# Turning the attention keys by 32 x 32 blocks on VectorE in a kernel of linear attention and two MLP layers

## The chip, the cores and the metric

One Trainium2 chip, one of its cores. The time is the device time of one launch in microseconds. The kernel before takes 914.3 us, the median of three runs (913.77 to 916.93).

## The reference

Linear attention with a decaying state (4 batches B, 8 heads H, 768 steps S, head size D of 48), then two MLP layers over the 3072 x 384 result, with a hidden width of 2048. Cut to what is computed:

```python
for t in range(S):                      # state: B, H, D, D
    cur = einsum('bhd,bhe->bhde', u * k[t], v[t])
    y[t] = einsum('bhd,bhde->bhe', r[t], state + cur)
    state = w[t][..., None] * state + einsum('bhd,bhe->bhde', k[t], v[t])
x = y.transpose(0, 2, 1, 3).reshape(B * S, H * D)        # 3072 x 384
h = x @ w_in;   x = (h * clip(h + 3, 0, 6) / 6) @ w_out  # layer 1
h = x @ w_in2;  x = (h * sigmoid(h)) @ w_out2            # layer 2
```

The MLP weights arrive as 64-bit floats, seen as pairs of 32-bit words, and are turned into 32-bit floats on the chip.

## The kernel before

**Groups and chunks.** The 768 steps are cut into 6 chunks of 128. A chunk of one batch is a group: 24 groups, group g being batch g % 4 of chunk g // 4. `attention(g, key)` (L588) handles one group with its 8 heads as 4 pairs, a pair on partitions 0 to 47 and 64 to 111 of a tile. Per group:

- VectorE scans the decay ws forward into `pre` (L600) and backward into `suf` (L607; `indq` between them is a reciprocal of four values), and multiplies them with r and k from `rk`: `rh` (L612), `kh` (L615).
- TensorE forms the scores `pa` of kh and rh (L625, 16 products), and turns kh with four matmuls against the identity into `pk` (L638). ScalarE copies pk to `khn` (L642).
- `bb` holds the sums of r u k by head. In groups 0 to 3 VectorE multiplies r and k (`rkp`, L646), and TensorE sums them against `u_bd` (L653). Later, GpSimd makes `ruk` (L659) and VectorE sums it (L666).
- ScalarE writes two tiles `a` that hold bb on their diagonals (L680), and VectorE puts pa above the diagonal with a masked copy (L683).
- TensorE forms the outputs `py` from the state, a and v (L696). ScalarE copies them to x (L714), and VectorE takes the rest that the copy lost (L717; not in chunk 0).
- For the state, TensorE multiplies khn and v to `pkv` (L728). The state `s` becomes (s + pkv) x `grown`, where grown is a copy of four columns of pre (L734). This is done on VectorE (L745, L746), and in groups 0 to 3 by eight activations on ScalarE (L754).

The last chunk (groups 20 to 23) needs no new state, so no pk, khn or pkv.

**MLP layers.** The four groups of a chunk are 512 tokens. `block1` (layer 1) and `block2` (layer 2) go over 16 slices fc of the hidden width. `mm1` makes h (L831) and `mm2` adds to three output sums, acc in layer 1 and acd in layer 2 (L851). Each product is made of three: both factors are split into a rounded part and a rest (wh, wl; xh, xl; gh, gl), so 9 matmuls for h and 9 for the sums. In chunk 0, the first 8 slices use the unsplit weights and x ("whole"; L821, L842), one matmul each. Between the two products ScalarE applies Relu (L882) or Silu (L921), VectorE the min and product (L884), a cast makes gh (L861 or L862, on either engine), and a subtraction on VectorE gl (L864).

**Weights.** `load_w` loads a slice's 64-bit words into `raw` (two buffers), VectorE decodes them in three steps (`upper_bits`, `sign_bits`, `lower_bits`), and ScalarE and VectorE split them (L488, L489) into one of 17 slots `w`. While these slots are empty, attention tiles of groups 1 to 3 live in them (names `spare` and `home`).

**What sets the order.** Nothing is scheduled by hand or by the compiler: every piece is an `Op` with a cost in ns for each engine that may run it, a key, and the tiles that it reads and writes. `Plan.order` is a list scheduler. It simulates the five engines, one DMA channel, the buffers, and a port that VectorE and GpSimd share (`port=True`), takes again and again the op that can start first (the lowest key among those), and writes out a fixed order for each engine. All DMAs are issued from SyncE's queue in this order. So a changed cost moves instructions elsewhere. `keep_busy` adds filler matmuls with a very high key, which run on TensorE before the first weight matmul where nothing else is ready. Groups 0 to 3 have keys below -96 and run first; groups 4 j to 4 j + 3 run among the MLP work of chunk j - 1.

Of the kernel before, what the change touches and what calls it, by code (L numbers as in the profile page):

```python
# [344 lines left out]
def tile_decay_attention_mlp2(  # L345
# [81 lines left out]
    indq = Part(ap_.tile([PD, SEQ + 1], F32, name="indq"))  # L427
    causal = Part(ap_.tile([128, C], F32, name="causal"))
    u_bc = Part(ap_.tile([128, H, D], F32, name="u_bc"))
    u_bd = Part(ap_.tile([PD, NP, 2], F32, name="u_bd"))  # L430
    stray = Part(stray_t)

    def fill_ind(e):
# [18 lines left out]
    wts, vals = {}, {}  # L452
    WBUFS = 17

    def load_w(layer, fc, key, where="wp", after=(), whole=False):
        src = (m1, m2)[layer]
        nm = f"{layer}_{fc}"
        raw = Part(new("cst", "raw", 2, [128, 2, DM, WW], f"raw{nm}", I32))
        op({"SP": 470}, key - 3, lambda e: e.dma_start(
            out=raw.ap.rearrange("p a f t -> p (a f t)"), in_=src[fc]  # L460
        ), writes=[raw], data=1150.0 * WW, after=after)
        if whole:
            if fc % 2 == 0:
                vals[fc] = new("wp", "w", WBUFS, [128, 2, 2, DM], f"val{nm}")
            val = Part(vals[fc - fc % 2], lambda t: t[:, fc % 2])
            bits = val
        else:
            bits = Part(new("cst", "bits", 1, [128, 2, DM], f"bits{nm}"))
            val = bits
        if WW == 2:  # L470
            op({"DVE": 480}, key, lambda e: upper_bits(e, raw.ap, val.ap.bitcast(I32)), [raw], [val])
# [62 lines left out]
    def load_group(g, key, after=()):  # L534
        first = 0 < g < B
        slots = {}

        def home(tag, shape, at, slot, kind="wp"):
            if not first or g == 1 and tag != "rk":
                return Part(new("np", tag, 1 if tag == "rk" else 2, shape, f"{tag}{g}"))  # L540
            if slot not in shared:
                shared[slot] = new("wp", "w", WBUFS, [128, 4 * DM], f"home{slot}")
            n = 1
            for x in shape[1:]:
                n *= x
# [10 lines left out]
        parts = [(ws, wseq_in, 700.0), (rk, rk_in, 1400.0), (vn, v_in, 700.0)]  # L556
        rkn = None
        if g >= B:
            rkn = Part(new("np", "rkn", 2, [128, 2 * H, D], f"rkn{g}"))
            parts.append((rkn, rkn_in, 1200.0))  # L560
        for p, src, data in parts:
            op({"SP": 470}, key, lambda e, p=p, src=src: e.dma_start(
                out=p.ap.rearrange("p a b -> p (a b)") if len(p.ap.shape) == 3 else p.ap,
                in_=src[g],
            ), writes=[p], data=data, after=after)
        return ws, rk, vn, rkn
# [8 lines left out]
            op({"PE": cost}, 1e6, run, [ident], [filler])  # L575

    filler = Part(new("ps", "h", 2, [128, 256], "filler"))
    keep_busy(16, 430)
    keep_busy(24, 300)

    states = {}
    x_parts = {}
    first_scores = []
# [4 lines left out]
    def attention(g, key):  # L588
# [7 lines left out]
        def of(t, i, n):  # L596
            return t.ap[:, i * n:(i + 1) * n, :]
# [10 lines left out]
            flat(suf)[:, ::-1], ws.ap[:, 1:SEQ + 1][:, ::-1], indq.ap[:, 1:SEQ + 1][:, ::-1],  # L608
            0.0, op0=ALU.mult, op1=ALU.add,
        ), [ws, indq], [suf], port=True)  # L610
        rh, kh = att("rh", [PD, NP, C], g), att("kh", [PD, NP, C], g)
        op({"DVE": 610}, key, lambda e: e.tensor_tensor(  # L612
            rh.ap, of(rk, 0, NP), pre.ap[:, :, 0:C], op=ALU.mult
        ), [rk, pre], [rh], port=True)
        op({"DVE": 610}, key, lambda e: e.tensor_tensor(  # L615
            kh.ap, of(rk, 1, NP), suf.ap[:, :, 1:SEG], op=ALU.mult
        ), [rk, suf], [kh], port=True)

        pa = [att_ps([128, NP, C], f"pa{i}_", g) for i in range(2)]
# [10 lines left out]
        o_scores = op({"PE": 1090}, key, scores, [kh, rh], pa)  # L630
        if g == 2:
            first_scores.append(o_scores)
        if not last:
            pk = att_ps([128, NP, PD], "pk", g)

            def back(e):
                for p in range(NP):
                    e.transpose(pk.ap[:, p, :], kh.ap[:, p, :], ident.ap[:PD, :PD])  # L638

            op({"PE": 500}, key, back, [kh, ident], [pk])  # L640
            khn = att("khn", [128, NP, PD], g)
            op({"ACT": 490}, key, lambda e: e.activation(khn.ap, pk.ap, AF.Copy), [pk], [khn])  # L642

        if first:
            rkp = att("rkp", [PD, NP, C], g)
            op({"DVE": 600}, key - 0.05, lambda e: e.tensor_tensor(  # L646
                rkp.ap, of(rk, 0, NP), of(rk, 1, NP), op=ALU.mult
            ), [rk], [rkp], port=True)
            bb = att_ps([128, H, 1], "bb", g)

            def sums(e):
                for p in range(NP):
                    e.matmul(bb.ap[:, 2 * p:2 * p + 2, 0], rkp.ap[:, p, :], u_bd.ap[:, p, :],  # L653
                             start=True, stop=True)

            op({"PE": 790}, key - 0.05, sums, [rkp, u_bd], [bb])
        else:
            ruk = att("ruk", [128, H, D], g)
            op({"POOL": 1000}, key, lambda e: e.tensor_tensor(  # L659
                ruk.ap, of(rkn, 0, H), u_bc.ap, op=ALU.mult  # L660
            ), [rkn, u_bc], [ruk], port=True)
            op({"POOL": 1000}, key, lambda e: e.tensor_tensor(
                ruk.ap, ruk.ap, of(rkn, 1, H), op=ALU.mult
            ), [ruk, rkn], [ruk], port=True)
            bb = Part(new("ap", "bb", 2, [128, H, 1], f"bb{g}"))
            op({"DVE": 540}, key, lambda e: e.tensor_reduce(  # L666
                flat(bb), ruk.ap, axis=AX.X, op=ALU.add
            ), [ruk], [bb])
# [6 lines left out]
        for i in range(2):  # L675
            a = att("a", [128, NP, C], g, str(i), bufs=2)

            def diagonal(e, a=a, i=i):
                for p in range(NP):
                    e.activation(a.ap[:, p, :], ident.ap, AF.Copy, scale=bs.ap[:, 2 * p + i])  # L680

            op({"ACT": 1000}, key, diagonal, [bs, ident], [a])
# [31 lines left out]
        op({"ACT": 490}, key, lambda e: e.activation(xh.ap[:, :, sl], py.ap, AF.Copy), [py], [xh])  # L714
        if j not in WHOLE:
            xl, = xl
            op({"DVE": 560}, key, lambda e: e.tensor_tensor(  # L717
# [3 lines left out]
        if not last:  # L721
# [3 lines left out]
            def outer_kv(e):  # L725
# [5 lines left out]

            op({"PE": 500}, key, outer_kv, [khn, vn], [pkv])
            grown = Part(new("ap", "grown", 2, [PD, NP, 1], f"grown{g}"))
            op({"DVE": 100}, key, lambda e: e.tensor_copy(grown.ap, pre.ap[:, :, C:SEG]),  # L734
               [pre], [grown])
            now = state
            if not state:
                now = Part(new("ap", f"s{o}", 1, [PD, NP, 2 * D], f"s{g}"))
# [19 lines left out]
            if state:  # L758
                op({"DVE": 1440}, key, grow, [pkv, now, grown], [now], port=True)
            else:  # L760
                op({"ACT": 1700}, key + 2.0, first_grow, [pkv, now, grown], [now])
            states[o] = now


# [70 lines left out]
            op({"PE": 681}, key, run, [wh, wl, xh, xl], [h])  # L835
        return h

    def mm2(layer, fc, gh, gl, acc, key):
        wh, *wl = wts[layer, fc]
        for c in range(KC):  # L840
            if not wl:
# [70 lines left out]
    def block2(j, key):  # L912
# [4 lines left out]
        for fc in range(FC):  # L917
# [2 lines left out]
            g = Part(new("gp", "g", 2, [128, N], f"g2_{j}_{fc}"))  # L920
            op({"ACT": 595}, kk, lambda e, g=g, h=h: e.activation(g.ap, h.ap, AF.Silu), [h], [g])  # L921
            gh, gl = split(g, f"2_{j}_{fc}", kk, {"DVE": 430}, {"DVE": 690})
            mm2(1, fc, gh, gl, acc, kk + MM2)
        for c in range(KC):
            o = Part(new("late", "o", 3, [128, N], f"o{j}_{c}"))
            op({"ACT": 595, "DVE": 690}, key + FC, lambda e, c=c, o=o: (
# [167 lines left out]
```

## Time and profile before

| | |
|---|---|
| median of the runs | 914.3 us |
| the profiled execution | 914.26 us |
| its span (first to last instruction) | 912.5 us |
| mean granted TensorE clock | 0.996 of full speed |
| HBM read, written | 90.75 MB, 9.44 MB: 110 GB/s |
| share of the chain that ended last: TensorE, VectorE, DMA, ScalarE | 88%, 8%, 2%, 1% |

In the profile PE is TensorE's matmul, PEld its weight load (which overlaps matmuls), DVE is VectorE, ACT ScalarE, POOL GpSimd and SPq the DMA queue of SyncE. The ends of pipelined matmuls are modelled, so for TensorE the distance between two starts is the surer figure. A row of a timeline gives the start and duration in us, the engine, the line, the operation and the tiles (out<-in), the shapes and how many instructions of one kind stand together; in brackets how long the engine was idle before, and for what. A name such as x, w or h stands for all its numbered buffers.

### The profile page before, as it was taken

What the parts mean: (1) busy time and instruction counts of PE and PEld (TensorE: products, weight loads), DVE (VectorE), ACT (ScalarE), POOL (GpSimd) and SP (SyncE); (2) the same over time, 40 slices, a digit from 0 to 9 for tenths busy, and PEclk for the clock granted to TensorE, in tenths of its full rate; (3) what the DMA queues carried; (4) which work ended last, traced back from release to release, by engine and by line L of the source; (5) the groups of instructions that cost most, each with busy time, mean ns of one, the idle gap of its engine ahead of it and who ended that gap; (6) DMA issues with size and microseconds to landing.
All of it is one profiled execution on the core that took longest, in us unless ns stands there. A gap on an engine that the chain in (4) does not pass through costs nothing.

```text
span 912.5 us, 13679 instructions
## 1 busy us (share of the span) xinstructions
PE 902.0 (99%) x5554; PEld 720.6 (79%) x5554; DVE 574.4 (63%) x942; ACT 324.6 (36%) x694; POOL 61.8 (7%) x52
## 2 busy tenths in 40 slices
PE   8999999999999999999999999999999999999997
PEld 7546788887888888888888888888888888888886
DVE  8999999867785776664468878544544633222221
ACT  5524474423432333322146765323232311212111
POOL 1203112311120211000000000000000000000000
PEclk9999999999999999999999999999999999999999
DMA  9765433322321221110066764634645500100101
GB/s 277 235 214 185 133 109 117 97 65 93 88 87 29 96 69 41 66 32 1 24 226 215 229 215 168 239 112 167 208 139 173 173 1 1 35 1 5 31 1 36
DMA packets 39603, 101.10 MB, mean 111 GB/s; under 512 B 3697, under 2 KB 16113, under 8 KB 39537
## 3 DMA queue, kind: packets, MB, share of 16 engines
q1 hardware_dynamic: 39536, 100.20, 34.2%
q8 instruction: 44, 0.72, 0.3%
q14 instruction: 23, 0.18, 0.1%
HBM read 90.75 MB, written 9.44 MB: 110 GB/s over the span
## 4 chain that ended last, share of the span: by engine, by line
PE 88%; DVE 8%; DMA 2%; ACT 1%; issue 1%; SPq 0%; DVEq 0%; ACTq 0%
PE h L831 40%; PE acd L851 21%; PE acc L851 19%; PE py L696 3%; PE pa L625 2%; PE pk L638 1%; DVE val L38 1%; DMA raw<-in_moe_w_dram 1%; PE pkv L728 1%; DVE g L884 1%; DVE bits L44 1%; DVE bits L38 1%; DVE val L44 1%; DVE pre L600 1%; DVE suf L607 0%
## 5 line engine op out<-in xcount | busy, mean ns | idle before, releaser
L831 PE MATMUL h<-x,w 128*128 128x512 f32 x1584 | 391.3, 390 | 0.0
L831 PEld LDWEIGHTS h<-x,w 128*128 128x128 f32 x1584 | 296.0, 188 | 62.2 <-issue 0.6
L851 PE MATMUL acd<-gh,w 128*128 128x512 f32 x576 | 192.9, 389 | 0.0
L862 DVE CAST gh<-g 128x512 fp32r<-128x512 f32 x150 | 64.9, 433 | 197.8 <-ACT g L921 194.2
L851 PE MATMUL acc<-gh,w 128*128 128x512 f32 x528 | 180.6, 393 | 0.3 <-ACT x L891 0.3
L921 ACT ACTIVATE g<-h 128x512 f32<-128x512 f32 x96 | 57.4, 599 | 264.3 <-PE h L831 242.8
L864 DVE TENSOR_TENSOR gl<-g,gh 128x512 fp32r<-128x512 f32 x184 | 130.1, 707 | 4.7 <-ACT gh L861 0.3
L851 PEld LDWEIGHTS acd<-gh,w 128*128 128x128 f32 x576 | 108.1, 188 | 22.3
L882 ACT ACTIVATE g<-h 128x512 f32<-128x512 f32 x96 | 57.2, 596 | 190.0 <-PE h L831 172.9
L851 PEld LDWEIGHTS acc<-gh,w 128*128 128x128 f32 x528 | 99.1, 188 | 22.8 <-issue 1.0
L884 DVE SCALAR_TENSOR_TENSOR g<-g,h 128x512 f32<-128x512 f32 x96 | 65.3, 682 | 77.6 <-ACT g L882 77.3
L851 PE MATMUL acd<-gl,w 128*128 128x512 f32 x288 | 112.1, 389 | 0.0
L851 PE MATMUL acc<-gl,w 128*128 128x512 f32 x264 | 103.1, 391 | 0.0
L851 PEld LDWEIGHTS acd<-gl,w 128*128 128x128 f32 x288 | 54.1, 188 | 11.3
L851 PEld LDWEIGHTS acc<-gl,w 128*128 128x128 f32 x264 | 49.6, 188 | 10.2 <-DVE gl L864 0.5
L659 POOL TENSOR_TENSOR ruk<-rkn,u_bc 128x384 f32<-128x384 f32 x20 | 36.1, 1807 | 288.4 <-DVE bb L666 250.1
L680 ACT ACTIVATE a<-ident,bb 128x128 f32<-128x128 f32 x160 | 49.6, 390 | 3.2 <-DVE bb L666 3.2
L683 DVE COPY_PREDICATED a<-causal,pa 128x512 f32<-128x512 int32 x42 | 29.1, 731 | 8.0 <-PE pa L625 8.0
L789 DVE TENSOR_SCALAR_CACHE_REDUCE cval<-cval 128x768 f32<-128x768 f32 x32 | 30.3, 946 | 2.3 <-ACT cval L28 2.3
L773 ACT ACTIVATE off<-cw 112x512 f32<-112x512 f32 x48 | 30.3, 631 | 1.8 <-DMA cw<-in_wseq_dram 0.9
L28 ACT ACTIVATE cval<-craw 128x768 f32<-128x768 f32 x32 | 28.8, 901 | 0.0
L600 DVE TENSOR_TENSOR_SCAN pre<-ws,ind 112x516 f32<-112x516 f32 x21 | 26.5, 1263 | 1.9 <-DMA ws<-in_wseq_dram 1.9
(105 smaller groups left out, 714.5 us busy)
## 6 DMA issues: line engine op xcount, KB each, us to landing
raw<-in_moe_w_dram SPq DMA_DIRECT2D x32, 768.0 KB, 4.7
craw<-in_moe_w_dram SPq DMA_DIRECT2D x32, 768.0 KB, 4.4
rk<-in_rk_dram SPq DMA_DIRECT2D x21, 448.0 KB, 3.9
rkn<-in_rkn_dram SPq DMA_DIRECT2D x20, 384.0 KB, 3.2
cw<-in_wseq_dram SPq DMA_DIRECT2D x24, 226.2 KB, 3.4
ws<-in_wseq_dram SPq DMA_DIRECT2D x22, 226.2 KB, 2.8
vn<-in_vn_dram SPq DMA_DIRECT2D x22, 224.0 KB, 2.6
x2d<-x SPq DMA_DIRECT2D x18, 256.0 KB, 2.4
```

Of the source, the lines that this page charges most:

```text
L600: op({"DVE": 1150}, key, lambda e: e.tensor_tensor_scan(flat(pre), ws.ap[:, 0:SEQ], ind.ap[:, 0:SEQ], 0.0, op0=ALU.mult, op1=ALU.add), [ws ...
L659: op({"POOL": 1000}, key, lambda e: e.tensor_tensor(ruk.ap, of(rkn, 0, H), u_bc.ap, op=ALU.mult), [rkn, u_bc], [ruk], port=True)
L680: e.activation(a.ap[:, p, :], ident.ap, AF.Copy, scale=bs.ap[:, 2 * p + i])
L773: e.activation(off.ap, ws.ap[:, 0:SEQ].rearrange("p (a b) -> p a b", b=SEG)[:, :, 1:], AF.Relu, scale=sign, bias=-W_REACH - sign, accum_ou ...
L789: op({"DVE": 600}, key, lambda e: e.tensor_scalar(val.ap, val.ap, TINY, 0.0, op0=ALU.is_lt, op1=ALU.add, accum_out=stray.ap[:, col:col + 1 ...
L831: e.matmul(h.ap, a.ap[:, 0, kc * 128:(kc + 1) * 128], b.ap[:, kc, :], start=(kc == 0 and i == 0), stop=(kc == KC - 1 and i == 2),)
L851: e.matmul(acc[c].ap, a.ap[:, 1, sl], b.ap, start=(fc == 0 and i == 0), stop=(fc == FC - 1 and i == 2),)
L862: else e.tensor_copy(gh.ap, src.ap)
L864: op(lo_engs, key, lambda e: e.tensor_tensor(gl.ap, src.ap, gh.ap.bitcast(F32), op=ALU.subtract), [src, gh], [gl], port=True)
L882: op({"ACT": 595}, kk, lambda e, g=g, h=h: e.activation(g.ap, h.ap, AF.Relu, bias=3.0), [h], [g])
L884: op({"DVE": 690}, kk, lambda e, g=g, h=h: e.scalar_tensor_tensor(g.ap, g.ap, 6.0, h.ap, op0=ALU.min, op1=ALU.mult), [g, h], [g])
L921: op({"ACT": 595}, kk, lambda e, g=g, h=h: e.activation(g.ap, h.ap, AF.Silu), [h], [g])
```

## The change

- For groups 9 to 19 the four matmuls pk and the copy khn go. VectorE transposes kh into khn with 16 instructions a group, each turning one 32 x 32 block of each of the four pairs (`turn`). For this kh has 128 partitions; ScalarE zeroes the upper 32. `TURN_FROM = 9` sets the first such group.
- In groups 4 to 8 the sums bb go from one VectorE reduction to eight activations with an accumulator on ScalarE (`total_by_head`). The copies `grown` go from VectorE to ScalarE in all groups.
- In layer 1, raw words of slices 2 to 9 are loaded into free slots w, up to four slices ahead.
- The first 24 instead of 16 fillers, of two matmuls each, are planned at 330 ns instead of 430.
- The buffer of u_bd is taken through the plan, and the first DMA is planned 450 ns longer; group 3's state is planned behind its copy of py to x.
- In the last chunk of layer 2, the keys of the last three slices' output sums are changed, so that the sums end one after another.
- Some planned durations of DMAs, of the diagonals and of upper_bits are changed.

```diff
@@ load_w
+    RAW_AHEAD = 4
+    def new_raw(layer, fc):
+        nm = f"raw{layer}_{fc}"
+        if layer == 0 and 2 <= fc < 10:
+            return Part(new("wp", "w", WBUFS, [128, 4 * DM], nm), ...)
+        return Part(new("cst", "raw", 2, [128, 2, DM, WW], nm, I32))
-        raw = Part(new("cst", "raw", 2, [128, 2, DM, WW], f"raw{nm}", I32))
+        if layer == 0:
+            for x in range(fc, min(fc + RAW_AHEAD, FC)):
+                if x not in raws:
+                    raws[x] = new_raw(0, x)
+        raw = raws.pop(fc) if layer == 0 else new_raw(layer, fc)
@@ fillers
-    keep_busy(16, 430)
+    keep_busy(24, 330)
     keep_busy(24, 300)
+    TURN_FROM = 9
@@ attention
-        rh, kh = att("rh", [PD, NP, C], g), att("kh", [PD, NP, C], g)
+        rh, kh = att("rh", [PD, NP, C], g), att("kh", [128 if g < 1 or g >= B else PD, NP, C], g)
+        if g >= TURN_FROM and not last:
+            op({"ACT": 500}, key, lambda e: e.activation(
+                kh.ap[96:], ident.ap[96:].unsqueeze(1).to_broadcast([32, NP, C]), AF.Copy, scale=0.0
+            ), [ident], [kh])
...
-        if not last:
+        if not last and g >= TURN_FROM:
+            khn = att("khn", [128, NP, 128], g)
+
+            def turn(e, i, j):
+                e.transpose(
+                    khn.ap[j * 32:(j + 1) * 32, :, i * 32:(i + 1) * 32],
+                    kh.ap[i * 32:(i + 1) * 32, :, j * 32:(j + 1) * 32],
+                )
+
+            for i in range(4):
+                for z in range(4):
+                    op({"DVE": 195}, key, lambda e, i=i, z=z: turn(e, i, z), [kh], [khn])
+        elif not last:
             pk = att_ps([128, NP, PD], "pk", g)
...
-            op({"DVE": 540}, key, lambda e: e.tensor_reduce(
-                flat(bb), ruk.ap, axis=AX.X, op=ALU.add
-            ), [ruk], [bb])
+            def total_by_head(e):
+                for h in range(H):
+                    e.activation(ruk.ap[:, h], ruk.ap[:, h], AF.Copy, accum_out=bb.ap[:, h])
+
+            if g < 9:
+                op({"ACT": 1900}, key, total_by_head, [ruk], [ruk, bb])
+            else:
+                op({"DVE": 540}, key, lambda e: e.tensor_reduce(
+                    flat(bb), ruk.ap, axis=AX.X, op=ALU.add
+                ), [ruk], [bb])
...
-            op({"DVE": 100}, key, lambda e: e.tensor_copy(grown.ap, pre.ap[:, :, C:SEG]),
-               [pre], [grown])
+            op({"ACT": 200}, key, lambda e: e.activation(
+                grown.ap, pre.ap[:, :, C:SEG], AF.Copy
+            ), [pre], [grown])
...
-                op({"ACT": 1700}, key + 2.0, first_grow, [pkv, now, grown], [now])
+                op({"ACT": 1700}, key + 2.0, first_grow, [pkv, now, grown], [now],
+                   after=[o_x] if g == B - 1 else ())
@@ block2
-            mm2(1, fc, gh, gl, acc, kk + MM2)
+            turn = {FC - 3: (-0.5, 0.05, 0.1), FC - 2: (0.2, 0.3, 1.4), FC - 1: (1.2, 1.3, 1.5)}
+            mm2(1, fc, gh, gl, acc, kk + MM2, [
+                key + FC - 1 + x for x in turn.get(fc, ())
+            ] if j == NCH - 1 else ())
```

The order of the instructions moves in three places that matter below. VectorE's queue in the head, before (group 0's scan, then its products; `spare1` and `home1` belong to group 1):

```order
L600 SCALAR_TENSOR_TENSOR pre_0_142<-ws0_101,ind_84 112x516
L603 RECIPROCAL indq_85<-pre_0_142 112x4
L734 COPY grown0_155<-pre_0_142 112x4
L646 TENSOR_TENSOR rkp_0_157<-rk0_109 112x512
L607 SCALAR_TENSOR_TENSOR suf_0_165<-ws0_101,indq_85 112x516
L612 TENSOR_TENSOR rh_0_177<-rk0_109,pre_0_142 112x512
L615 TENSOR_TENSOR kh_0_190<-rk0_109,suf_0_165 112x512
```

and in the changed kernel:

```order
L617 SCALAR_TENSOR_TENSOR pre_0_148<-ws0_99,ind_84 112x516
L620 RECIPROCAL indq_85<-pre_0_148 112x4
L624 SCALAR_TENSOR_TENSOR suf_0_165<-ws0_99,indq_85 112x516
L679 TENSOR_TENSOR rkp_0_180<-rk0_103 112x512
L633 TENSOR_TENSOR rh_0_186<-rk0_103,pre_0_148 112x512
L636 TENSOR_TENSOR kh_0_195<-rk0_103,suf_0_165 112x512
```

The copy of grown has gone, and the backward scan stands ahead of rkp, the first instruction that needs rk. VectorE's queue in chunk 1, between the masked copy of group 9 and the rest gl of slice 4, before:

```order
L683 COPY_PREDICATED a1_9_1609<-causal_86,pa1_9_1629 128x512
L884 SCALAR_TENSOR_TENSOR g1_4_1637<-g1_4_1637,h0_1_4_1603 128x512
L603 RECIPROCAL indq_85<-pre_10_1639 112x4
L666 TENSOR_REDUCE bb10_1699<-ruk_10_1599 128x8
L607 SCALAR_TENSOR_TENSOR suf_10_1703<-ws10_1391,indq_85 112x516
```

and in the changed kernel, where slice 4 is handled:

```order
L658 STREAM_TRANSPOSE khn_9_1660<-kh_9_1503 32x4x32
L930 SCALAR_TENSOR_TENSOR g1_4_1743<-g1_4_1743,h0_1_4_1688 128x512
L658 STREAM_TRANSPOSE khn_9_1660<-kh_9_1503 32x4x32
L908 CAST gh1_4_1767<-g1_4_1743 128x512
L658 STREAM_TRANSPOSE khn_9_1660<-kh_9_1503 32x4x32
L910 TENSOR_TENSOR gl1_4_1773<-g1_4_1743,gh1_4_1767 128x512
L658 STREAM_TRANSPOSE khn_9_1660<-kh_9_1503 32x4x32
L707 TENSOR_REDUCE bb10_1782<-ruk_10_1647 128x8
L658 STREAM_TRANSPOSE khn_9_1660<-kh_9_1503 32x4x32
L930 SCALAR_TENSOR_TENSOR g1_5_1779<-g1_5_1779,h0_1_5_1755 128x512
```

Nearly every transposition stands between two instructions of other kinds, and the cast gh is on VectorE. TensorE's queue at group 12, before:

```order
L625 MATMUL pa0_12_2244<-rh_12_2092,kh_12_2034 128x128
L625 MATMUL pa1_12_2246<-rh_12_2092,kh_12_2034 128x128
L638 MATMUL pk12_2256<-ident_83,kh_12_2034 128x112 x4
L831 MATMUL h0_2_0_2262<-x0_0_2_1519,w0_0_1312 128x512
L831 MATMUL h0_2_0_2262<-x1_0_2_1535,w0_0_1312 128x512
```

and in the changed kernel:

```order
L646 MATMUL pa0_12_2328<-rh_12_2187,kh_12_2240 128x128
L646 MATMUL pa1_12_2330<-rh_12_2187,kh_12_2240 128x128
L875 MATMUL h0_2_0_2341<-x0_0_2_1557,w0_0_1382 128x512
L875 MATMUL h0_2_0_2341<-x1_0_2_1582,w0_0_1382 128x512
L875 MATMUL h0_2_0_2341<-x0_0_2_1557,w0_0_1382 128x512 x2
```

The four turning matmuls pk12 have gone, and the weight matmuls follow the scores.

## Rows read from the trace of the kernel before

**Rows 1.** The page, part 1: busy us, share of the span and instructions.

```profile
PE 902.0 (99%) x5554; PEld 720.6 (79%) x5554; DVE 574.4 (63%) x942; ACT 324.6 (36%) x694; POOL 61.8 (7%) x52
```

**Rows 2.** Timeline of TensorE, 29 to 33 us; start and duration first.

```profile
30.43 1.08 PE L696 MATMUL py<-spare,home 128*32 128x128 f32 x32
...
32.57 0.70 PE L821 MATMUL h<-x,val 128*128 128x512 f32 x1 [0.73 <-ACT x L714]
```

**Rows 3.** Timeline of TensorE, its last weight matmul.

```profile
906.48 0.39 PE L851 MATMUL acd<-gh,w 128*128 128x512 f32 x1
```

**Rows 4.** Timeline of VectorE, 4 to 14 us.

```profile
4.19 1.23 DVE L600 TENSOR_TENSOR_SCAN pre<-ws,ind 112x516 f32<-112x516 f32 x1 [1.94 <-DMA ws<-in_wseq_dram]
...
5.94 0.69 DVE L646 TENSOR_TENSOR rkp<-rk 112x512 f32<-112x512 f32 x1 [0.25 <-DMA rk<-in_rk_dram]
...
11.47 1.34 DVE L683 COPY_PREDICATED a<-causal,pa 128x512 f32<-128x512 int32 x2 [0.57 <-PE pa L625]
```

**Rows 5.** Timeline of SyncE's DMA queue, its first issue.

```profile
0.81 0.41 SPq L944 DMA_DIRECT2D u_bd<-in_u_pairs_dram  x1
```

**Rows 6.** Timeline of TensorE, 1.4 to 12.7 us.

```profile
1.44 4.21 PE L572 MATMUL filler<-ident 128*128 128x256 bf16 x24 [1.44 <-POOL ident masks.py:199]
...
9.26 2.08 PE L625 MATMUL pa<-rh,kh 48*128 48x128 f32 x16
...
11.70 1.04 PE L572 MATMUL filler<-ident 128*128 128x256 bf16 x8
```

**Rows 7.** Timeline of TensorE around pk of groups 9 and 19.

```profile
145.68 1.16 PE L625 MATMUL pa<-rh,kh 48*128 48x128 f32 x16
146.77 0.60 PE L638 MATMUL pk<-ident,kh 112*128 112x112 f32 x4
147.15 0.48 PE L851 MATMUL acc<-gh,w 128*128 128x512 f32 x1
...
341.73 0.55 PE L638 MATMUL pk<-ident,kh 112*128 112x112 f32 x4
342.21 0.32 PE L696 MATMUL py<-rh,s 112*32 112x128 f32 x4
```

**Rows 8.** Windows: us, busy of PE, PEld, DVE, ACT, POOL, clock, DMA share, GB/s.

```profile
8.00:9.00 1.00, 1.00 (x7) 0.60 (x4) 1.00 (x3) 0.94 (x4) 0.00 (x0) 0.50 1.05 287
```

**Rows 9.** Groups by line and form, VectorE: busy us, mean ns; idle before.

```profile
L734 DVE COPY grown<-spare 112x4 f32<-112x4 f32 x3 | 0.4, 147 | 0.0
```

**Rows 10.** Timeline of ScalarE, 30 to 33 us.

```profile
30.27 1.73 ACT L754 ACTIVATE s<-pkv,grown 48x48 f32<-48x48 f32 x8 [0.72 <-POOL ruk L659]
32.02 0.49 ACT L714 ACTIVATE x<-py 128x384 f32<-128x384 f32 x1
```

**Rows 11.** Timeline of TensorE, 93.2 to 93.9 us, behind attention matmuls.

```profile
93.24 0.50 PE L831 MATMUL h<-xh,w 128*128 128x512 f32 x1
93.58 0.40 PE L831 MATMUL h<-xl,w 128*128 128x512 f32 x1
```

**Rows 12.** Timeline of all engines, 899.8 to 902.9 us.

```profile
899.84 0.69 DVE L864 TENSOR_TENSOR gl<-g,gh 128x512 fp32r<-128x512 f32 x1
...
902.57 0.39 PE L851 MATMUL acd<-gh,w 128*128 128x512 f32 x1
...
902.80 0.39 PE L851 MATMUL acd<-gl,w 128*128 128x512 f32 x1
```

**Rows 13.** Timeline of VectorE, 135 to 136.2 us.

```profile
135.09 0.36 DVE L746 TENSOR_TENSOR s<-s,grown 48x192 f32<-48x192 f32 x1
135.46 0.56 DVE L717 TENSOR_TENSOR x<-py,x 128x384 fp32r<-128x384 f32 x1
135.93 0.95 DVE L489 TENSOR_TENSOR w<-val,w 128x768 fp32r<-128x768 f32 x1
```

**Rows 14.** Windows, the stretch 127.7 to 294.6 us; columns as in rows 8.

```profile
127.70:294.60 166.90, 166.56 (x1399) 134.68 (x1398) 127.56 (x216) 61.42 (x147) 28.11 (x22) 1.00 0.28 86
```

**Rows 15.** Groups by line and form, ScalarE: busy us, mean ns; idle before.

```profile
L773 ACT ACTIVATION_READ_ACCUMULATOR off<-cw 112x1 f32 x48 | 9.0, 188 | 0.0
```

More of the change, by code (lines that the diff above doesn't have):

```diff
@@ L429, in tile_decay_attention_mlp2 @@
     u_bc = Part(ap_.tile([128, H, D], F32, name="u_bc"))
-    u_bd = Part(ap_.tile([PD, NP, 2], F32, name="u_bd"))
+    u_bd = Part(new("ap", "u_bd", 1, [PD, NP, 2], "u_bd"))
     stray = Part(stray_t)
@@ L453, in tile_decay_attention_mlp2 @@
     WBUFS = 17
+    raws = {}
+    RAW_AHEAD = 4
+    def new_raw(layer, fc):
+        nm = f"raw{layer}_{fc}"
+        if layer == 0 and 2 <= fc < 10:
+            return Part(new("wp", "w", WBUFS, [128, 4 * DM], nm), lambda t: (
+                t.bitcast(I32).rearrange("p (a f t) -> p a f t", a=2, t=WW)
+            ))
+        return Part(new("cst", "raw", 2, [128, 2, DM, WW], nm, I32))
     def load_w(layer, fc, key, where="wp", after=(), whole=False):
@@ L457, in load_w @@
         nm = f"{layer}_{fc}"
-        raw = Part(new("cst", "raw", 2, [128, 2, DM, WW], f"raw{nm}", I32))
+        if layer == 0:
[3 more added lines that the diff above has]
+        raw = raws.pop(fc) if layer == 0 else new_raw(layer, fc)
         op({"SP": 470}, key - 3, lambda e: e.dma_start(
             out=raw.ap.rearrange("p a f t -> p (a f t)"), in_=src[fc]
-        ), writes=[raw], data=1150.0 * WW, after=after)
+        ), writes=[raw], data=1500.0 * WW, after=after)
         if whole:
@@ L470, in load_w @@
         if WW == 2:
-            op({"DVE": 480}, key, lambda e: upper_bits(e, raw.ap, val.ap.bitcast(I32)), [raw], [val])
+            op({"DVE": 480}, key, lambda e: upper_bits(e, raw.ap, val.ap.bitcast(I32)),
+               [raw], [val], port=True)
             for step in (sign_bits, lower_bits):
@@ L555, in load_group @@
         vn = home("vn", [128, NP, ED], 2 * NP * C, g)
-        parts = [(ws, wseq_in, 700.0), (rk, rk_in, 1400.0), (vn, v_in, 700.0)]
+        parts = [(ws, wseq_in, 850.0), (rk, rk_in, 1650.0), (vn, v_in, 760.0)]
         rkn = None
@@ L559, in load_group @@
             rkn = Part(new("np", "rkn", 2, [128, 2 * H, D], f"rkn{g}"))
-            parts.append((rkn, rkn_in, 1200.0))
+            parts.append((rkn, rkn_in, 1100.0))
         for p, src, data in parts:
@@ L615, in attention @@
         op({"DVE": 610}, key, lambda e: e.tensor_tensor(
-            kh.ap, of(rk, 1, NP), suf.ap[:, :, 1:SEG], op=ALU.mult
+            kh.ap[:PD], of(rk, 1, NP), suf.ap[:, :, 1:SEG], op=ALU.mult
         ), [rk, suf], [kh], port=True)
@@ L637, in back @@
                 for p in range(NP):
-                    e.transpose(pk.ap[:, p, :], kh.ap[:, p, :], ident.ap[:PD, :PD])
+                    e.transpose(pk.ap[:, p, :], kh.ap[:PD, p, :], ident.ap[:PD, :PD])
             op({"PE": 500}, key, back, [kh, ident], [pk])
-            khn = att("khn", [128, NP, PD], g)
-            op({"ACT": 490}, key, lambda e: e.activation(khn.ap, pk.ap, AF.Copy), [pk], [khn])
+            khn = att("khn", [128, NP, 128 if g < 1 or g >= B else PD], g)
+            op({"ACT": 490}, key, lambda e: e.activation(khn.ap[:, :, :PD], pk.ap, AF.Copy), [pk], [khn])
         if first:
@@ L680, in diagonal @@
                     e.activation(a.ap[:, p, :], ident.ap, AF.Copy, scale=bs.ap[:, 2 * p + i])
-            op({"ACT": 1000}, key, diagonal, [bs, ident], [a])
+            op({"ACT": 1230 if first else 1550}, key, diagonal, [bs, ident], [a])
             op({"DVE": 610}, key, lambda e, a=a, pa=pa[i]: e.copy_predicated(
@@ L713, in attention @@
         sl = slice(o * C, (o + 1) * C)
-        op({"ACT": 490}, key, lambda e: e.activation(xh.ap[:, :, sl], py.ap, AF.Copy), [py], [xh])
+        o_x = op({"ACT": 490}, key, lambda e: e.activation(xh.ap[:, :, sl], py.ap, AF.Copy),
+                 [py], [xh])
         if j not in WHOLE:
@@ L836, in mm1, with mm2 @@
         return h
-    def mm2(layer, fc, gh, gl, acc, key):
+    def mm2(layer, fc, gh, gl, acc, key, late=()):
         wh, *wl = wts[layer, fc]
         for c in range(KC):
+            if c < len(late):
+                key = late[c]
             if not wl:
@@ L942, in tile_decay_attention_mlp2 @@
     begun = [o for o in plan.ops if "SP" in o.engs]
+    begun[0].data += 450.0
     for p, src, k in ((u_bd, ub_in, 0.2), (u_bc, u_in, B + 0.5)):
```

## The prediction

> **What bounds the kernel now.** I read the page first, then TensorE's timeline, then VectorE's. TensorE is busy for 902.0 of 912.5 us [rows 1]. Its matmul ends are modelled, so I looked at starts instead: from the first weight matmul at 32.57 us [rows 2] to the last of the output chain at 906.48 us [rows 3], the matmuls follow one another nearly without a pause. The time is therefore three parts: a head of 32.6 us before the first weight matmul, about 874 us of queued TensorE work, and a tail of some 6 us (906.87 to 912.5). The profiled execution took 914.26 us, 1.8 us more than its span; the three runs have a median of 914.3, so the sum is made against 914.3. A change of under 0.5% (4.6 us) can't be told from none here.
>
> **Head.** In the chain before the first weight matmul VectorE is the one that is waited for. It starts its first scan at 4.19 us when ws lands [rows 4]; ws is second in SP's queue, behind the issue of u_bd, which takes 0.41 us [rows 5]. The new order puts u_bd behind ws, rk and vn: 0.4 us earlier. The 0.25 us for rk in front of rkp [rows 4] goes because suf, which needs no rk, now stands there. The 0.57 us in front of the first masked copy at 11.47 us [rows 4] is a wait for the scores pa, and those took 2.08 us at 9.26 us [rows 6] against 1.16 for the same eight products at 145.68 [rows 7]: the granted clock was 0.50 there [rows 8], that is 1.2 GHz, after TensorE had stood from 5.65 us (24 filler matmuls, 1.44 + 4.21) to about 6.7. Now 40 fillers stand there; at the later fillers' 0.13 us (8 in 1.04, [rows 6]) 16 more end near 7.7 us, so TensorE no longer stands, and I take the 0.57 us as gone. Four grown copies of 0.147 us [rows 9] leave VectorE, three or four of them in this chain: 0.4. Last, the copy of py into x that releases the first weight matmul now goes ahead of the state scaling s on ScalarE: py ended at 31.51 (30.43 + 1.08, [rows 2]), the copy ran at 32.02 behind s [rows 10]: 0.5. Together 2.1 us. ScalarE now carries grown as well and its diagonals end only some tenths before VectorE asks for them, so I take 2.0; the bounds are 0 (ScalarE or the small u_bd, now behind 0.9 MB, becomes the late one) and 2.1.
>
> **TensorE work that goes.** For groups 9 to 19 the four turning matmuls pk disappear. From start to next start they take 0.38 us in the first of the eleven (146.77 to 147.15) and 0.48 in the last (341.73 to 342.21) [rows 7]; seven are like the first and four like the last: 4.5 us, all on the path. Against that, the new order breaks the attention work into more pieces between the weight matmuls: after the first weight matmul there are 50 stretches of attention matmuls instead of 45. Coming out of one, the first weight matmul takes 0.34 us (93.24 to 93.58, [rows 11]) where one in the steady rhythm takes 0.23 (902.57 to 902.80, [rows 12]): 0.1 each, 0.5, say 0.6 us with the way in. Net 3.9 us.
>
> **VectorE work that comes.** This is the term that decides. 11 groups x 16 = 176 block transpositions of 32 x 4 x 32, 128 elements per partition; no row shows one. Below: a copy of 4 elements takes 0.147 us [rows 9], and where an instruction overlaps the next by 0.09 us, as x does at 135.46 (0.56 us, next start after 0.47, [rows 13]), only 0.06 us of it would count. Above: the s update with 192 elements, 0.36 us [rows 13]. A line between the two gives 0.147 + 124/188 x 0.213 = 0.287 us for 128 elements, and 0.197 with the overlap. The planner is told 0.195. Which of the two holds is read from the s row: at 135.09 s works on the partitions from 64 on, the next instruction, x, starts at partition 0, and it starts 0.37 us later, after the full 0.36: no overlap although the order shows no wait between them. Fifteen of the sixteen transpositions read or write another 32-partition block than their neighbour, so they are nearest to that row: 0.287 us.
>
> What it costs: from 127.7 to 294.6 us VectorE is busy 127.56 of 166.9 us [rows 14]. The new order puts 135 transpositions there (the stretch from g1_0 to g3_0); the other exchanges about cancel (nine grown copies go, six casts gh come back from ScalarE). The stretch itself gets 3.3 - 0.4 us shorter, 164.0. At 0.287 us: 127.6 + 38.7 = 166.3, 2.3 us more than fits. Slack: a gl that ends at 900.53 (899.84 + 0.69) is first read at 902.80, its gh at 902.57 [rows 12], so 2.0 us of lateness are free in the steady rhythm, but VectorE can't run at 100% with its waits on ScalarE and TensorE. I charge 2.5 us; the bounds are 0 (overlapping: 127.6 + 26.6 = 154.2, 94% full) and 12.5 (below).
>
> **ScalarE and the rest.** The sums bb of groups 4 to 8 become eight activations with an accumulator. Such a read takes 0.188 us [rows 15], an activation of 48 elements 0.216 (s, 8 in 1.73, [rows 10]): 3.2 us per group where the planner is told 1.9, and ScalarE's Relu of the weight products waits behind it. TensorE has two h buffers and the 2 us above; I charge 0.1 us per group, 0.5 (bounds 0 and 5 x 1.3 = 6.5). The zeroing of kh's rows 96 to 127 replaces the khn copy that goes: nothing. The weight loads that go ahead into free slots end a wait of VectorE for raw, but TensorE had no gap there that the chain shows: nothing, bounds 0 and a gain of 1.
>
> **Tail.** In the last block the three output sums now end c0, c1, then six matmuls for c2. c2 ends when it did; c0 and c1 leave three matmuls (0.7 us) earlier, so the last transfer finds the queue emptier; what follows the last matmul (906.87 us, [rows 3]) is one copy, one transfer and the end of the program. I take 0.3 us, bounds 0 and 0.7.
>
> **Sum.** 914.3 - 2.0 (head) - 3.9 (TensorE) + 2.5 (VectorE late) + 0.5 (ScalarE) - 0.3 (tail) = 911.1 us.
>
> **Rivals.**
> 1. *The transpositions hide.* They overlap like other VectorE work, 0.195 us, VectorE is 94% full and TensorE never waits for them. For it: the stretch as a whole has 39.3 us of idle VectorE time [rows 14]. Against it: the s row. 911.1 - 2.5 = 908.6 us.
> 2. *VectorE becomes the bound (slower).* Each transposition also takes the overlap from the instruction behind it: 0.287 + 0.09 = 0.377 us, 135 of them 50.9. 127.6 + 50.9 = 178.5 against 164.0: 14.5 over, less the 2.0 of slack is 12.5: 908.6 + 12.5 = 921.1 us. For it: the order alternates nearly every transposition with one on partition 0. Against it: about half of these stand between an instruction and the one that waits for its result, where there was no overlap to lose. It turns the change into a loss once the price passes (164.0 + 2.0 + 5.7 - 127.6) / 135 = 0.326 us. The Trainium skill has this as a rule, "VectorE: DVE Perf Modes", section "Two Vector instructions with no wait between them": an instruction whose input or output starts in another quadrant than the last one's is held until every earlier Vector instruction has finished. By that rule the trace agrees as far as one row goes (135.09 to 135.46, 0.37 us).
> 3. *The head stays.* ScalarE or u_bd is what VectorE and TensorE wait for, and none of the 2.0 us is gained: 913.1 us. For it: ScalarE takes the grown copies in front of diagonals that VectorE needs. Against it: u_bd and the diagonals are due only after rkp and the scores.
>
> The same page, section "The three transpose paths", gives VectorE 311 ns for 128x128 in bf16. By that figure the 135 would take 42.0 us and the sum would be about 3 us higher (an estimate); no run here shows one yet.
>
> **How the numbers follow.** Forecast 0.42 (its own range 908.5 to 913.5), rival 1 0.30 (907 to 909.7), rival 2 0.18 (914 to 923), rival 3 0.08, anything else 0.02. Faster by over 0.5% means under 909.7: most of rival 1 (0.28) and a quarter of the forecast (0.11), 0.39. Slower by over 0.5% means over 918.9: two thirds of rival 2 and the rest, 0.13. Within 0.5%: 0.48. The range 907 to 918.5 leaves out some 0.03 below and 0.14 above.
>
> **What would show it.** Right: the first weight matmul at about 30.5 us, pa of group 0 at about 1.2 us and no 0.5 clock there; no pk after group 8; a transposition near 0.28 us and the next instruction no earlier than its end; VectorE near full between 125 and 290 us and TensorE's waits there for gl, g or the masked copies some 2.5 us in all. Transpositions that start 0.2 us apart and an idle share of VectorE of 5% there would show rival 1; waits of over 8 us there, rival 2. A first weight matmul at 32 us or later would show rival 3. The forecast is wrong if the first half (to 295 us) isn't the place where the time changes: from 517 us on nothing but the last 15 us is touched.

## The result: slower, 927.0 us

The changed kernel takes 927.0 us (median of 4, 925.8 to 927.7) where the kernel before takes 914.6: ratio 1.0132, interval 1.0116 to 1.0147. The forecast was 911.1 and its range ended at 918.5. The profiled execution took 927.66 us, its span 925.9. Where the 13.4 us between the two profiled executions arise shows in the start of Relu or Silu of some slices (us):

| slice | before | after minus before |
|---|---|---|
| chunk 0, slice 0 | 35.4 | -1.4 |
| chunk 1, slice 0 | 125.2 | -1.9 |
| chunk 1, slice 8 | 170.3 | +1.0 |
| chunk 2, slice 0 | 211.3 | +4.5 |
| chunk 2, slice 8 | 252.7 | +7.9 |
| chunk 3, slice 0 | 293.7 | +12.6 |
| chunk 4, slice 0 | 372.6 | +13.2 |
| layer 2, from its second chunk on | 580.2 | +13.3 to 13.4 |

So 14.5 us are lost in chunks 1 and 2, where the forecast had looked. The window of that stretch in the changed kernel (columns as in [rows 8]; its counterpart before is [rows 14]):

```profile
126.20:306.30 180.10, 172.32 (x1376) 134.04 (x1375) 170.51 (x345) 59.97 (x143) 21.25 (x20) 0.99 0.26 78
```

VectorE's busy time, 170.5 of 180.1 us, still looks as if there were room. Counted from start to start there is none: adding up, for each VectorE instruction, the distance to the next start (cut at 0.12 us past its end) gives 178.2 us, and 1.8 us idle. Before, the same sum over [rows 14] is 134.4, not the 127.6 of busy time: pauses of some 0.03 us between one instruction's end and the next one's start are idle by the busy time. What TensorE then waits for, by its waits in the whole run:

```profile
PE pkv L770 <- DVE khn L658: 5.7, 6, 1.4
PE h L875 <- DVE g L930: 1.9, 3, 1.1
PE acc L897 <- DVE gl L910: 1.5, 3, 0.8
```

Before, no wait of TensorE for VectorE behind the head is over 0.3 us. The waits named make 9 us, 7.4 of them between slice 0 of chunk 1 and of chunk 3; for the rest of what is lost there the trace names no wait. One cluster of them costs twice. Windows (columns as in [rows 8]): TensorE stands for half of the first stretch, and then runs at a granted clock of 0.50 (1.2 GHz):

```profile
196.80:200.90 4.10, 2.03 (x22) 1.08 (x20) 3.90 (x10) 0.99 (x2) 0.00 (x0) 1.00 0.00 1
201.40:204.30 2.90, 2.90 (x8) 2.31 (x7) 2.71 (x6) 0.00 (x0) 1.87 (x2) 0.50 0.31 85
```

Eight weight matmuls stand there 0.43 us apart instead of 0.23: another 1.6 us.

VectorE's timeline shows what the new instructions do:

```profile
140.91 0.29 DVE L658 STREAM_TRANSPOSE khn<-kh 32x128 f32<-32x128 f32 x1
141.13 1.05 DVE L908 CAST gh<-g 128x512 fp32r<-128x512 f32 x1
...
144.19 0.30 DVE L658 STREAM_TRANSPOSE khn<-kh 32x128 f32<-32x128 f32 x1
144.52 0.74 DVE L724 COPY_PREDICATED a<-causal,pa 128x512 f32<-128x512 int32 x1
145.30 0.30 DVE L658 STREAM_TRANSPOSE khn<-kh 32x128 f32<-32x128 f32 x1
```

The first of group 9's transpositions, block 0 to block 0, is followed after 0.22 us, before its end. The later ones, between different blocks, are followed after 0.33 us, past their end, and the masked copy between them gives way after 0.78 us, also past its end. Over the stretch a transposition takes 0.322 us from start to start (134 in 43.1 us), a masked copy 0.72 (0.62 before).

### The profile page after: what moved, and what is told of

It reads as the page before. It is cut to its first block, busy times and chain, and to the rows that moved or that the text cites. A ratio compares the mean times of both kernels' runs of the same rounds, so it can differ in the third digit from the quotient of the medians.

```text
span 925.9 us, 13885 instructions
## 1 busy us (share of the span) xinstructions
PE 907.2 (98%) x5526; PEld 718.5 (78%) x5526; DVE 630.4 (68%) x1104; ACT 331.9 (36%) x783; POOL 59.8 (6%) x52
## 4 chain that ended last, share of the span: by engine, by line
PE 70%; DVE 26%; issue 2%; ACT 1%; POOL 0%; ACTq 0%; DVEq 0%; POOLq 0%
PE h L875 33%; PE acd L897 21%; PE acc L897 11%; DVE khn L658 5%; DVE g L930 3%; DVE gl L910 3%; DVE pre L617 2%; DVE a L724 2%; DVE gh L908 2%; DVE suf L624 1%; PE py L737 1%; PE pa L646 1%; DVE s L789 1%; DVE rh L633 1%; DVE kh L636 1%
## 5 line engine op out<-in xcount | busy, mean ns | idle before, releaser
L908 DVE CAST gh<-g 128x512 fp32r<-128x512 f32 x163 | 71.8, 440 | 195.1 <-ACT g L967 191.8
L897 PE MATMUL acc<-gh,w 128*128 128x512 f32 x528 | 183.4, 397 | 0.3 <-DVE gh L908 0.3
L910 DVE TENSOR_TENSOR gl<-g,gh 128x512 fp32r<-128x512 f32 x184 | 128.1, 696 | 5.0 <-ACT gh L907 0.3
L897 PEld LDWEIGHTS acd<-gl,w 128*128 128x128 f32 x288 | 54.1, 188 | 11.1
L658 DVE STREAM_TRANSPOSE khn<-kh 32x128 f32<-32x128 f32 x176 | 53.2, 302 | 4.4 <-PE pkv L770 0.2
L692 POOL TENSOR_TENSOR ruk<-rkn,u_bc 128x384 f32<-128x384 f32 x20 | 31.3, 1566 | 309.0 <-DVE bb L707 254.0
```

Of the source, the lines that this page charges most:

```text
L658: e.transpose(khn.ap[j * 32:(j + 1) * 32, :, i * 32:(i + 1) * 32], kh.ap[i * 32:(i + 1) * 32, :, j * 32:(j + 1) * 32],)
L692: op({"POOL": 1000}, key, lambda e: e.tensor_tensor(ruk.ap, of(rkn, 0, H), u_bc.ap, op=ALU.mult), [rkn, u_bc], [ruk], port=True)
L897: e.matmul(acc[c].ap, a.ap[:, 1, sl], b.ap, start=(fc == 0 and i == 0), stop=(fc == FC - 1 and i == 2),)
L908: else e.tensor_copy(gh.ap, src.ap)
L910: op(lo_engs, key, lambda e: e.tensor_tensor(gl.ap, src.ap, gh.ap.bitcast(F32), op=ALU.subtract), [src, gh], [gl], port=True)
```

## The experiments

**The turning or the rest.** Two runs part the change. The changed kernel without the turning:

```diff
-    TURN_FROM = 9
+    TURN_FROM = 99
```

> The changed kernel, but TensorE turns the keys of all groups (TURN_FROM = 99), the rest of the change stays. Theory F (VectorE is full): in the changed kernel VectorE stands idle for only 1.8 us between 126.2 and 306.3 us, and the 134 transpositions there take 43.1 us from start to start, so the loss is theirs alone. Then this run keeps the 1.4 us that the head gained and pays the pk matmuls again: 913.1 us (911.5 to 914.5). Theory R (the rest of the change costs: sums on ScalarE, raw words in free slots): 920 us or more.

Measured: 912.9 us, 0.9986 (0.9976 to 0.9996). And the kernel before with the turning alone (`turn`, kh of 128 rows and ScalarE's zeroing, as in the change):

> The kernel before with the turning on VectorE alone added, from group 9 on. Theory F: VectorE's demand between the first slices of chunks 1 and 3 is 134.4 us from start to start before, plus 135 transpositions at 0.32 to 0.37 us, plus some 3 us of casts that move to it, 181 to 187 us where TensorE has some 163 us of work; with the grown copies and the sums still on VectorE it is slower than the changed kernel by 1 to 5 us: 928 to 932 us. Theory R: 911 to 915 us, since the turning by itself costs nothing.

Measured: 932.3 us, 1.0213 (1.0195 to 1.0230). The loss is the turning's; the rest gains about 1.3 us. R falls.

**The price.** A row of VectorE instructions behind the kernel's end:

```diff
...
+        for x in range(12):
+            t(0, 0, x % 4)
+        for x in range(12):
+            t(0, x % 4, x // 4)
+        for x in range(8):
+            t(0, 0, x % 4)
+            full()
+        for x in range(8):
+            t(1, 2, x % 4)
+            full()
...
```

`t(i, j, z)` turns a block from partition block i into partition block j; `full` is a product of 128 x 512.

> The kernel before with a row of VectorE instructions added behind its last output transfer, for their prices from start to start; nothing else uses VectorE there, and the time of this run means nothing. In the changed kernel a transposition lasts 0.302 us and the next instruction starts 0.322 us after it. Theory H (what costs is the change of partition block): transpositions within block 0 one behind the other start some 0.06 to 0.1 us closer (0.20 to 0.25 us) than those whose output block changes (0.30 to 0.33 us); a 128 x 512 product behind a transposition from block 1 to block 2 costs the transposition its full 0.30 us, one behind a transposition in block 0 less. Theory P (the price is the instruction's own): about 0.30 us in all of them, and a product of 48 partitions starts no closer to one of the same partitions than to one of the others.

Its timeline of VectorE, a stretch of each pattern in this order:

```profile
912.02 2.41 DVE L988 STREAM_TRANSPOSE mdst<-msrc 32x128 f32<-32x128 f32 x12
...
914.66 3.81 DVE L988 STREAM_TRANSPOSE mdst<-msrc 32x128 f32<-32x128 f32 x12
...
918.98 0.29 DVE L988 STREAM_TRANSPOSE mdst<-msrc 32x128 f32<-32x128 f32 x1
919.20 0.64 DVE L994 TENSOR_TENSOR moth<-msrc 128x512 f32<-128x512 f32 x1
919.77 0.29 DVE L988 STREAM_TRANSPOSE mdst<-msrc 32x128 f32<-32x128 f32 x1
...
925.70 0.30 DVE L988 STREAM_TRANSPOSE mdst<-msrc 32x128 f32<-32x128 f32 x1
926.03 0.69 DVE L994 TENSOR_TENSOR moth<-msrc 128x512 f32<-128x512 f32 x1
926.75 0.30 DVE L988 STREAM_TRANSPOSE mdst<-msrc 32x128 f32<-32x128 f32 x1
```

Within one block: 0.20 us each (2.41 / 12). With a changing output block: 0.32 (3.81 / 12). A pair of transposition and product takes 0.79 us within block 0 (918.98 to 919.77) and 1.05 across (925.70 to 926.75): 0.11 us more for the transposition, 0.15 for the product behind it. In both patterns the products carry a wait and the transpositions, but for the first ones, none, so the difference isn't one of waits. H holds. The planner's 195 ns is the price within one block; in the changed kernel's order the price is 0.33 us, or 0.48 with what the next instruction loses. By the Trainium skill, "VectorE: DVE Perf Modes", section "Two Vector instructions with no wait between them", an instruction whose input or output starts in another quadrant than the last one's starts only once all before it have finished; these rows agree with it. (The part with products of 48 partitions tells nothing: they all write the same tile, and each waited for the one before.)

**The price inside the kernel.** The changed kernel in nearly its own order, but all transpositions within block 0 (and ScalarE zeroes khn instead of kh's upper rows; not shown):

```diff
...
-                    khn.ap[j * 32:(j + 1) * 32, :, i * 32:(i + 1) * 32],
-                    kh.ap[i * 32:(i + 1) * 32, :, j * 32:(j + 1) * 32],
+                    khn.ap[0:32, :, i * 32:(i + 1) * 32],
+                    kh.ap[0:32, :, j * 32:(j + 1) * 32],
...
```

> The changed kernel in its own order, but every transposition reads and writes partitions 0 to 31 (blocks 0 to 0), so the turned keys are not put where they belong; ScalarE zeroes khn instead of the rows of kh. Same number and size of transpositions, planned at the same 195 ns. Theory H (the price is the change of partition block): in the run that measured prices a transposition from block 0 to block 0 and a product behind it took 0.225 + 0.570 us, from block 1 to block 2 0.334 + 0.723 us. Here 134 transpositions should then cost some 13 us less themselves and their neighbours up to 8 us less, VectorE needs about 157 to 165 us in the stretch from chunk 1 to chunk 3, and the time is 908 to 913 us. Theory D (any 176 instructions more in VectorE's queue make its results late, whatever their blocks): 920 us or more.

Measured: 911.5 us, 0.9970 (0.9960 to 0.9979). D falls: as many instructions in nearly the same places, 15.5 us less (14.8 by the two ratios). VectorE between slice 0 of chunk 1 and of chunk 3, by windows, first of the changed kernel, then of this one (columns as in [rows 8]):

```profile
123.30:306.30 183.00, 175.22 (x1388) 136.46 (x1388) 173.41 (x349) 62.87 (x147) 21.25 (x20) 0.99 0.26 77
```

```profile
123.30:292.70 169.40, 169.40 (x1388) 135.30 (x1387) 154.44 (x347) 61.92 (x147) 20.75 (x20) 1.00 0.28 83
```

The same number of instructions but for two, from start to start 180.9 and 160.7 us. The transpositions (134 and 130 of them) take 9.0 us less of it; the rest, 11.1 us, is the others' (min-and-product g 0.68 to 0.62 us, gl 0.69 to 0.62, masked copy 0.72 to 0.62). So between these two runs the hold shows in the neighbours as much as in the transpositions. But the others take 137.8 us in the changed kernel (214 instructions), 126.6 here (216), and 137.0 in the run without turning (216): without transpositions, too, they stand apart. Transpositions within one block fit into these pauses; those of the changed kernel don't.

**The planned price.** The same transpositions, told to the planner at other prices, first 320 ns, then 480 (`...` stands for the lambda):

```diff
-                    op({"DVE": 195}, key, ..., [kh], [khn])
+                    op({"DVE": 320}, key, ..., [kh], [khn])
```

> The changed kernel with a planned cost of 320 ns instead of 195 for each transposition; the instructions are the same, their order changes. Theory O (the order is wrong: planned too cheap, the last transposition of a group comes too late, and TensorE waits for khn, 5.7 us in all in the changed kernel's trace): the waits go, 912 to 918 us. Theory F: the planner can move only a few casts to ScalarE, VectorE needs about the same 0.32 to 0.37 us per transposition, 923 to 929 us.

> The changed kernel with a planned cost of 480 ns per transposition: the 0.334 us from its start to the next, and 0.153 us that the product behind it lost (0.723 against 0.570 us). Theory O (a plan with true prices loses little): the planner leaves the casts on ScalarE and spreads the attention work to the middle of chunk 4, so VectorE is not overfilled anywhere; 910 to 914 us, better than the 915.5 us with 320 ns. Theory F (VectorE's work is too much wherever it is put): no better than with 320 ns, 915 to 920 us.

Measured: 915.5 us, 1.0019 (1.0010 to 1.0029), and 912.9 us, 0.9993 (0.9984 to 1.0003). My theory F, that VectorE's sum is too much wherever it is put, falls; O holds. The price itself didn't change (0.302 us lasts one in all three traces). What changed is where the work stands: between slice 0 of chunks 1 and 3 the order has 135 transpositions and 25 casts gh on VectorE at 195 ns, 118 and 26 at 320, 107 and 6 at 480. The rest is done up to the middle of chunk 4 and on ScalarE. At 480, the only waits of TensorE for VectorE over 0.4 us are pa's for kh, 1.0 us in two, and VectorE's window is:

```profile
122.60:286.90 164.30, 163.98 (x1278) 131.18 (x1278) 147.83 (x284) 70.66 (x157) 18.09 (x16) 1.00 0.25 73
```

**In rows.** Sixteen transpositions as one piece at 5.1 us, so that only the last holds another kind up:

```diff
...
+            def turn_all(e):
+                for i in range(4):
+                    for z in range(4):
+                        turn(e, i, z)
+            op({"DVE": 16 * 320}, key, turn_all, [kh], [khn])
```

> The changed kernel with the 16 transpositions of a group one behind the other as one planned piece of 5.1 us. In a row they took 0.316 us each, and only the last holds another instruction up. Theory S (VectorE's sum decides): 135 x 0.13 us = 17 us less for its neighbours than in the changed kernel, 911 to 916 us. Theory L (lateness decides): a gl that arrives 5 us late is more than the 2.0 us that TensorE can do without it; some 3 us are lost in each of 11 groups, 935 to 945 us.

Measured: 918.5 us, 1.0057 (1.0041 to 1.0074), between the two. TensorE's waits there:

```profile
PE h L878 <- DVE g L933: 5.4, 5, 1.1
```

The waits for gl make another 1.0 us in two. A row of 5 us makes g and gl late, by about a microsecond at a time, not 3. Shorter rows, the first of four (1420 ns), the second of two (785 ns), the third of four but only for groups 16 to 19:

```diff
...
+            def turn_some(e, n):
+                for x in range(n, n + 4):
+                    turn(e, *divmod(x, 4))
+            for n in range(0, 16, 4):
+                op({"DVE": 1420}, key, lambda e, n=n: turn_some(e, n), [kh], [khn])
```

> The changed kernel with a group's 16 transpositions in four rows of four, each row planned at 1420 ns (4 x 0.316 + 0.153 us). Theory H: only the last of a row holds another instruction up, so a group costs VectorE 5.7 us instead of 16 x 0.487 = 7.8 us, and a row is shorter than the 2.0 us that a gl may be late; better than the 912.9 us of single transpositions at a true price: 910.5 to 912.5 us. Rival T (TensorE's own gain is what is small: without any lateness, with cheap transpositions, only 911.5 us were reached): 912.5 to 913.5 us, since the rows break up its work as before.

> As e9_fours, in rows of two at 785 ns (2 x 0.316 + 0.153 us): 6.3 us of VectorE per group. Theory H: between single ones (912.9 us) and rows of four: 911 to 913 us.

> As e9_fours, but turning on VectorE only for groups 16 to 19, whose work lies in the half of chunk 2 and chunk 3 where VectorE had 11 to 14 us of idle time in 40. Four groups give back some 4 x 0.45 = 1.8 us of pk, less the stretches. Theory H: 911.5 to 912.9 us, between no turning and e9_fours. If VectorE's room in the first chunks is what still costs, it is better than e9_fours.

Measured: 910.1 us, 0.9953 (0.9935 to 0.9971); 911.7 us, 0.9967 (0.9956 to 0.9979); 911.5 us, 0.9969 (0.9956 to 0.9982). T falls. The rows of four beat both kernels: they are clear of single transpositions at 480 ns (0.9984 to 1.0003), and 0.4 us below what H gave; fours, twos and the third run aren't apart from each other. VectorE of the fours, window and timeline:

```profile
122.90:291.40 168.50, 168.50 (x1388) 135.41 (x1388) 154.41 (x321) 77.71 (x175) 21.96 (x18) 1.00 0.26 78
```

```profile
160.07 2.50 DVE L658 STREAM_TRANSPOSE khn<-kh 32x128 f32<-32x128 f32 x8
```

Two rows stand together here (8 in 2.50 us, 0.31 each), and TensorE is busy in the whole window. The transpositions cost as much as in the changed kernel (0.322 us each over the window); the planner leaves only 2 casts gh on VectorE there, not 25, and the other 192 instructions together take 120.0 us.

**The head and the sums.** Without turning on VectorE, first with fewer fillers, then with the sums bb of groups 4 to 8 back on VectorE (B is 4):

```diff
-    keep_busy(24, 330)
+    keep_busy(24, 400)
```

> As e1_no_turn (no turning on VectorE), with the first 24 filler pieces planned at 400 ns instead of 330, so that some 34 instead of 40 of them stand ahead of bb. In the changed kernel 40 fillers ran to 8.5 us, bb, ready at 7.3 us, stood behind them, pa ran at 9.71 us and VectorE still waited 0.58 us for it. Theory: the fillers are now what is late; with fewer of them pa starts near 8.6 us at full clock and the wait goes: first weight matmul 0.3 to 0.6 us earlier than in e1_no_turn, 912.3 to 912.7 us. Rival: the clock falls again in the pause, pa takes 2.1 us as before the change, and nothing is gained: 912.9 us or more.

```diff
-            if g < 9:
+            if g < B:
```

> As e1_no_turn, with the sums of groups 4 to 8 back on VectorE. The prediction charged 0.5 us for them on ScalarE: then this run is 912.4 us. If the planner's move frees VectorE for more than it costs ScalarE, it is 913.2 us or more.

Measured: 913.8 us, 1.0004 (0.9994 to 1.0014), and 915.1 us, 1.0011 (1.0001 to 1.0022). The first did what it should in the head: pa at 8.91 us (9.13 without the edit), first weight matmul at 30.26 (30.63). But the order behind it came out worse: its lead over before, 2.4 us at slice 0 of chunk 0, is 0.1 at slice 0 of chunk 1, where the run without the edit still has 2.4. Neither theory speaks of that. The second is 2.2 us slower: it loses 3.7 us in the second half of chunk 0. There VectorE is busy for 41.11 of 41.40 us in the kernel before:

```profile
83.80:125.20 41.40, 41.07 (x324) 32.01 (x323) 41.11 (x63) 23.43 (x45) 6.76 (x4) 1.00 0.39 129
```

So five sums of 0.54 us more are not hidden there. How much of the 2.2 us is theirs and how much the order's stays open. A changed number moves the whole order, so a difference of one or two microseconds between two of these kernels is not the edit's alone.

## Why the prediction was wrong

1. **VectorE work that comes** is the step that failed: 2.5 us, with an upper bound of 12.5, where the run within block 0 against the changed kernel gives some 15. The s row [rows 13] was read rightly, and the hold was in the text; what it costs was counted too low in two places. I took 0.287 us for a transposition from its neighbours' durations, where 0.322 is what it holds VectorE for. And I took the others at 127.6 us [rows 14], their busy time; from start to start they take 134.4, and a held transposition doesn't fit into the difference. 134.4 + 43.1 = 177.5 against 164.0 is 13.5 us too much, not 2.3. Rival 2 is the mechanism that came, with 0.18: the 178.5 us that it gave VectorE are what VectorE took (178.2). Its time was 5.9 us short, about 3.0 because the hold cost 15.5 and not 12.5 (it had taken off 2.0 for slack), and 2.9 because even without the hold the kernel reached 911.5 us and not 908.6.
2. What the step did not ask: whether the order would be the same at the true price. I took it as given and compared sums; the planner had filled chunks 1 and 2 by a price of 0.195 us, and the room that VectorE has from the middle of chunk 3 to the end of chunk 4 (36 us from start to start) stayed empty. Told 480 ns, the change costs nothing.
3. **TensorE work that goes.** The 4.5 us were nearly right (attention matmuls 69.8 us without turning, 65.5 in the run within block 0: 4.3 gone). The 0.6 us for breaking up were too small: that run has 52 stretches of attention matmuls against 45, and 100 weight matmuls against 81 whose successor starts only after 0.3 us or a little more; these 19 make 2.0 us. Another 0.9 us are in its head, so it is only 1.4 us faster than the one without turning. In the rows of four, with 47 stretches and 90 such matmuls, 2.8 us remain.
4. **Head.** First weight matmul at 31.22 us, 1.35 earlier, not 2.0. The first scan, which waits for ws, started 0.21 us earlier (3.98 us), not 0.4; rk's wait went. The clock stayed up, and pa took 1.16 us, as forecast. But the 0.57 us stayed, with another cause: the fillers, forecast to end at 7.7 us, ran until 8.5, and bb (8.37 us) and pa (9.71) stood behind them. TensorE's timeline, then VectorE's:

```profile
1.44 7.09 PE L588 MATMUL filler<-ident 128*128 128x256 bf16 x40 [1.44 <-POOL ident masks.py:199]
```

```profile
11.00 0.73 DVE L724 COPY_PREDICATED a<-causal,pa 128x512 f32<-128x512 int32 x1 [0.58 <-PE pa L646]
```

The working gave each of the 16 more fillers 0.13 us, from the later ones; the first ones start every 0.213 us, up to a moment that isn't the order's (last section). With the same order in the head, the first weight matmul came at 30.63 us without turning and at 30.48 at 480 ns, which is the 2.0. Nor is all of it the change's: the kernel before with the turning alone has the head of the kernel before, instruction for instruction, but there the clock stayed up, pa took 1.16 us and the first weight matmul came at 31.77 us, 0.8 earlier than in [rows 2].
5. **ScalarE.** The sums there were charged 0.5 us, and taking them back costs 2.2: no loss shows, rather a gain, of which the order's share stays open. Their price was nearly right: 0.230 us for the activation and 0.189 for the read, 3.4 us per group.
6. **Tail.** Nothing of the 0.3 us: from the start of the last matmul to the end 6.0 us before [rows 3], 6.1 after (919.80 to 925.9).

## What to carry to other kernels

Count an engine's room from start to start and from its busy time, and ask which of the two the new instructions can use: here they differ by 7 us in 167, transpositions within one block used the difference, and those that change the block could not. Price a small VectorE instruction in the neighbourhood that it will have; one that changes its partition block costs itself and the next instruction their overlap, so put such instructions side by side, in short rows (four, of 1.3 us, gained; sixteen, of 5 us, made others late). Where a planner orders by costs, a wrong cost does harm twice, since the work also goes where it doesn't fit.

## What the hardware showed that was not expected

The fillers at the start run at two paces while the granted clock reads 1.00 in both: one starts every 0.213 us, later every 0.109. In the kernel before, fillers that run at a granted 0.50 (1.2 GHz; from 7.84 to 8.91 us, [rows 8]) also start every 0.213 us, so the reading of 1.00 doesn't show the pace of the first ones. When it changes differs from run to run: at 4.4 us in the kernel before, 6.7 in the changed one, 5.5 without turning, 7.4 in the run within block 0. The window of the changed kernel from 6 to 7 us (columns as in [rows 8]; the count takes in what lies there in part), and the same 40 fillers without turning, which took 6.51 us and not 7.09:

```profile
6.00:7.00 1.00, 1.00 (x8) 0.75 (x7) 1.00 (x2) 0.00 (x0) 0.00 (x0) 1.00 1.03 283
```

```profile
1.45 6.51 PE L588 MATMUL filler<-ident 128*128 128x256 bf16 x40 [1.45 <-POOL ident masks.py:199]
```

The head moved with it by up to 1.1 us: in nine runs with the same order there, the first weight matmul came between 30.48 us (pace changed at 4.6) and 31.57 (at 7.5), the later the later the pace changed. The row of sixteen is an exception (changed at 4.8, first weight matmul at 31.52).
